# Linear attention and an expert layer on one core: second half of kv ahead of the denominators in batch 0, more idle products, and weight sums five tiles earlier

## The chip, the cores and the metric

The kernel runs on one core of a Trainium2 chip. The core has five engines with queues of their own: TensorE (PE in the profile; its weight loads are PEld), VectorE (DVE), ScalarE (ACT), GpSimd (POOL) and SyncE (SP). They meet through semaphores. Operands lie in SBUF; PE writes its results into PSUM, which has eight banks. The metric is the device time of one execution in microseconds (us), and of several runs the median.

## What is computed

Linear attention on 8 batches of 8 heads, 576 tokens and 64 channels, and then a dense layer on the 4608 tokens of 512 channels, with 2048 hidden channels:

```
phi(x) = where(x > 0, x, exp(x) - 1) + 1
kv  = einsum('bhsd,bhse->bhde', phi(k), v)
z   = sum(phi(k), axis=2)
x   = einsum('bhsd,bhde->bhse', phi(q), kv) / (einsum('bhsd,bhd->bhs', phi(q), z) + 1e-6)
h   = x @ w_in
out = (h * sigmoid(beta * h)) @ w_out
```

Inputs and output are float32; the kernel multiplies in bfloat16.

## The kernel before

The order of all work is written out by hand: each engine runs its instructions in the order in which the source issues them, and the framework adds the semaphore waits that the data need. A tile pool with a tag hands out its buffers in turn; a new tile waits until the last readers of its buffer are through.

The work is a pipeline over batches. For each batch, attention gives x (in the code xs, a tile of 128 tokens at a time), x is transposed to xT, an H phase makes 16 f tiles of h (128 hidden channels each, on 512 tokens) with the activation on ACT into g, and a Y phase multiplies g with w_out. While H and Y of block b run on PE, DVE, ACT and POOL prepare the attention of batches b + 1 and b + 2. The main loop hangs these pieces into the phases through two tables, `sh` for H and `sy` for Y: `at(sh, 9, f)` runs f after the f tile with number 9. Blocks 3 and up use a fast scheme in H (`h_fast`) that needs sums of parts of w_in; these are made once, by `h_w_sums(0)` in block 2: four DVE additions (lines 783 to 786). In blocks 1 and 2 the H phase is the plain one (`h_phase`). There, beside it, DVE also takes `kv_both` (line 231 copies kv out of PSUM), `numer_all` (lines 346 to 348, scaling of numerators of the next batch) and `g_parts` (lines 725 to 731, sums of g for the Y phase, each as soon as the last f tile of its four is there).

Batch 0 has no earlier work to hide behind, so it has an order of its own:

- SP loads q and k of batch 0 in halves of four heads; POOL loads v in two halves, after a small copy (`gate`) that waits for the first half of q, and then all weights in a row.
- `idle(n)` issues n products of a constant tile with itself into a bank that nobody reads. They compute nothing that is used. They stand at the start and wherever PE waits.
- phi of q, half by half (`phi_part`: exp on ACT, lines 169 and 175 on DVE), then its transposes on PE (`q_half`, `q_last`), which are copied to qT. bps is beta, transposed on PE.
- phi of k, half by half, `z_sums` (line 516) and `kv_first` (line 527), both on PE; `kv_mask` (line 536, two DVE instructions for each half) keeps the blocks of kv that belong to one head.
- zbd (line 554, two DVE instructions) is z in the same block form. The denominators are 20 small products of qT with zbd (line 564, tile dps), and `denom` (lines 571 and 572, an addition and a reciprocal on DVE) inverts them: once for the tiles 0 to 3 together, once for the last tile of 64 tokens.
- `numer_first(t)` makes the numerators of tile t on PE (line 583) and scales them on DVE (line 587). `x_first(t)` transposes the result on PE (line 382), and ACT copies it to xT (line 239). `h_first(t)` makes the part of the first four f tiles that belongs to tile t (line 402).

Two PSUM pools of four banks are in use during that: `hps` (`bank`) and `fps` (`bank1`). In the order of the source, the second half of kv comes after all denominators:

```
kv_first(0); z_sums(1); idle(1)
kv_mask(0); zbd
20 denominators; kv_first(1)
denom(tiles 0-3); kv_mask(1)
numer_first(0..2); denom(tile 4); x_first(0); numer_first(3); x_first(1); h_first(0); ...
```

Later lines that the text names: line 410 is the activation that writes g, line 162 the exp of later batches, line 986 the products of the Y phase, lines 1009 and 1010 DVE's sums u of them, line 1047 the gate copy that stands before the loads of later batches.

Of the kernel before, what the change touches and what calls it, by code (L numbers as in the profile page):

```python
# [8 lines left out]
F32 = mybir.dt.float32  # L9
BF16 = mybir.dt.bfloat16  # L10
ALU = mybir.AluOpType
# [5 lines left out]
def kernel(  # L17
# [10 lines left out]
    nc = tc.nc  # L28
# [4 lines left out]
    P = 128  # L33
    KC = DM // P
    FC = DFF // P
    G = 64
    J = S // G
    NT = 5
# [6 lines left out]
    consts = ctx.enter_context(tc.tile_pool(name="consts", bufs=1))  # L45
# [5 lines left out]
    def bank(name, shape=None, dt=F32):  # L51
        return hps.tile(shape or [P, 512], dt, tag="h", name=name)

    def bank1(name, shape=None, dt=F32):
        return fps.tile(shape or [P, 512], dt, tag="f", name=name)
# [17 lines left out]
    warm = consts.tile([P, 512], BF16, name="warm")  # L73
# [73 lines left out]

    warm_ps = bank("warm_ps")

    def idle(n):  # L150
        for _ in range(n):
            nc.tensor.matmul(warm_ps, warm[:, 0:P], warm, start=True, stop=True)

    def table(func):
        nc.scalar.activation(act0, warm[:, 0:1], func)  # L155
# [2 lines left out]
    st = {}  # L158
# [23 lines left out]
    def xin(b, a, pr):  # L182
        if b == 0:
            return x0f[pr if a == "q" else 2 + pr]
        return (xk if a == "k" else xq)[b % 2][:, 2 * pr : 2 * pr + 2]

    def phi_part(b, a, pr):
        x = xin(b, a, pr)
        phi_exp(b, a, pr, x)
        phi_relu(b, a, pr, x)  # L190
        phi_min(b, a, pr)
# [17 lines left out]
    def half(hh):  # L209
        return slice(hh * G, (hh + 1) * G)  # L210
# [32 lines left out]
    def q_half(b, pr, tp):  # L243
        for j in range(8):
            nc.tensor.matmul(
                tp.rearrange("p (t h i g) -> p t h i g", t=4, h=2, i=2)[:, j // 2, :, j % 2, :],
                st[b, "q"][:, pr, j, :], identity,
                is_transpose=True, start=True, stop=True, skip_group_check=True,
            )
# [35 lines left out]
    def rows_of(t):  # L285
        return P if t < NT - 1 else G

    def xs_tile(b, t):
        st[b, "xs", t] = xs_sb.rearrange("p i n -> p (i n)")[:, t * DM : (t + 1) * DM]
        n = rows_of(t)  # L290
        return st[b, "xs", t][:n].rearrange("p (i a d) -> p a i d", a=2, d=D)
# [188 lines left out]
            nc.vector.tensor_sub(ws[k][:, r], a, b)  # L480


    idle(11)
    beta_c = consts.tile([P, FC], F32)
    beta_m = consts.tile([P, FC], F32)
    rbeta = consts.tile([P, FC], F32)
# [5 lines left out]
    qtp = [bank1("qtp", [P, 1024], BF16) for _ in range(2)]  # L492
    phi_part(0, "q", 0)
    q_half(0, 0, qtp[0])
    idle(3)
    phi_part(0, "q", 1)
    q_half(0, 1, qtp[1])
    t8 = bank1("qtp8", [P, 2 * P], BF16)
    q_last(0, t8)
    bps = bank("bps", [P, FC])  # L500
    nc.tensor.matmul(bps, beta_row, ident16, is_transpose=True, start=True, stop=True)
    idle(4)
    x = xin(0, "k", 0)
    phi_exp(0, "k", 0, x)
    phi_relu(0, "k", 0, x)
# [5 lines left out]
    zbd = consts.tile([P, 2, 2, 2], BF16)  # L511

    def z_sums(pr):
        for j in range(J):
            for hh in range(2):
                nc.tensor.matmul(
                    zps[hh][:, pr : pr + 1], st[0, "k"][half(hh), pr, j, :], ones[half(hh)],
                    start=(j == 0), stop=(j == J - 1), skip_group_check=True,
                )
# [4 lines left out]
    def kv_first(pr):  # L524
        for j in range(J):
            for hh in range(2):
                nc.tensor.matmul(
                    kvp0[hh][:, pr * P : (pr + 1) * P],
                    st[0, "k"][half(hh), pr, j, :],
                    v0b[half(hh), 2 * pr : 2 * pr + 2, j, :],  # L530
                    start=(j == 0), stop=(j == J - 1), skip_group_check=True,
                )

    def kv_mask(pr):
        for hh in range(2):
            nc.vector.tensor_mul(
                kv0[:, hh, pr].rearrange("p (h d) -> p h d", h=2),
                kvp0[hh][:, pr * P : (pr + 1) * P].rearrange("p (h d) -> p h d", h=2),
                kvmask[:, hh, :, 0:D],
            )  # L540

    z_sums(0)
    idle(1)
    phi_part(0, "k", 1)
    q_copy(nc.scalar, 0, 1, qtp[1])
    q_copy_last(nc.scalar, 0, t8)
# [2 lines left out]
    kv_first(0)  # L549
    z_sums(1)  # L550
    idle(1)
    kv_mask(0)
    for hh in range(2):
        nc.vector.tensor_mul(
            zbd[:, hh], zps[hh][:, 0:2, None].to_broadcast([P, 2, 2]), kvmask[:, :, :, 0]
        )
    dps = bank("dps", [P, NT, 2, 2, 2])
    den0 = consts.tile([P, NT, 8], F32)
    rden0 = consts.tile([P, NT, 8], F32)
    for t in range(NT):  # L560
        n = rows_of(t)
        for hh in range(2):
            for pr in range(2):
                nc.tensor.matmul(
                    dps[:n, t, hh, pr], st[0, "qT"][:, pr, t, hh, 0:n], zbd[:, hh, pr, :],
                    start=True, stop=True, skip_group_check=True,
                )
    dv = dps.rearrange("p t a b c -> p t (a b c)")

    def denom(r, ts):  # L570
        nc.vector.tensor_scalar(den0[:r, ts], dv[:r, ts], 1e-6, None, ALU.add)
        nc.vector.reciprocal(rden0[:r, ts], den0[:r, ts])

    kv_first(1)
    denom(P, slice(0, NT - 1))
    kv_mask(1)

    def numer_first(t):
        n = rows_of(t)
        nps = bank1("nps0", [P, 2, 2, P])  # L580
        for hh in range(2):
            for pr in range(2):
                nc.tensor.matmul(
                    nps[:n, hh, pr], st[0, "qT"][:, pr, t, hh, 0:n], kv0[:, hh, pr, :],
                    start=True, stop=True, skip_group_check=True,
                )
        nc.vector.tensor_mul(
            xs_tile(0, t),
            nps[:n].rearrange("p a b (c d) -> p a (b c) d", d=D),
            rden0[:n, t].rearrange("p (a i) -> p a i", a=2)[:, :, :, None].to_broadcast(  # L590
                [n, 2, 4, D]
            ),
        )
# [5 lines left out]
    hp0 = []  # L599

    def h_first(t):
        if not hp0:
            hp0.extend(bank("h_ps") for _ in range(4))
        for ff in range(4):
            h_mm(xT[0], ff, hp0[ff], t * P, (t + 1) * P)

    for t in range(3):
        numer_first(t)
    denom(G, slice(NT - 1, NT))
    x_first(0, nc.scalar)  # L610
    numer_first(3)
    x_first(1, nc.scalar)
# [107 lines left out]
    def at(side, n, *fs):  # L720
        side.setdefault(n, []).extend(fs)
# [58 lines left out]
    def h_w_sums(fq):  # L780

        s, a = h_w[fq], lambda f, r: h_w_plain(fq, f, r)
        nc.vector.tensor_add(s[:, 0], a(1, 0), a(1, 1))
        nc.vector.tensor_sub(s[:, 1], s[:, 0], a(0, 0))
        nc.vector.tensor_sub(s[:, 2], a(0, 0), a(1, 0))
        nc.vector.tensor_sub(s[:, 3], a(0, 1), s[:, 1])
# [267 lines left out]
    for b in range(1, B + 1):  # L1054
        n, m = b + 1, b + 2
        sh, sy = {}, {}
        if b == 2 or b == B - 1:
            at(sh, 0, lambda: tail_copy(b))
        if n < B:
            at(sh, 0, lambda: next_loads(n))  # L1060
            if b > 2:
                at(sh, 0, lambda: tail_copy(b))
            at(sh, {1: 9, 2: 3}.get(b, 0), lambda: kv_both(n))
            at(sh, {1: 11, 2: 6}.get(b, 10), lambda: numer_all(n))
        if b == 1:
            at(sh, 4, lambda: w_sum(2))
            at(sh, 9, lambda: w_sum(1))
            at(sy, 0, lambda: w_sum(3))
        if m < B:
            at(sy, 0, lambda: phi_tile(m, "q"), lambda: phi_tile(m, "k"))  # L1070
            if b == 1:

                for pr in range(2):
                    at(sy, 0, lambda pr=pr: v_copy(nc.scalar, m, pr))
                for pr in range(2):
                    at(sy, 0, lambda pr=pr: phi_exp(m, "q", pr, xin(m, "q", pr)))
                    at(sy, 3 + 2 * pr, lambda pr=pr: phi_relu(m, "q", pr, xin(m, "q", pr)))
                    at(sy, 4 + pr, lambda pr=pr: phi_min(m, "q", pr))
                at(sy, 5, lambda: q_trans_dma(m))
                for pr in range(2):  # L1080
                    at(sy, 5, lambda pr=pr: phi_exp(m, "k", pr, xin(m, "k", pr)))
                    at(sy, 5 + pr, lambda pr=pr: phi_relu(m, "k", pr, xin(m, "k", pr)))
                    at(sy, 6, lambda pr=pr: phi_min(m, "k", pr))
                at(sy, 6, lambda: table(ACTF.Silu))
            else:
                at(sy, 0, lambda: phi_part(m, "q", 0))
                at(sy, 1, lambda: phi_part(m, "q", 1))
                at(sy, 1, lambda: q_trans_dma(m))
                at(sy, 4, lambda: phi_part(m, "k", 0))
                at(sy, 4, lambda: phi_part(m, "k", 1), lambda: table(ACTF.Silu))  # L1090
        if b == 2:
            at(sh, 9, lambda: h_w_sums(0))
        if b == B - 2:
            at(sy, 4, lambda: h_w_sums(2))
        if 2 <= b < B:
            at(sy, 6 if b < B - 2 else 0, lambda: h_x_sums(n))
        (h_phase if b < 3 else h_fast)(b, xT[b % 2] if b < B else xT_tail, sh)
        y_fast(b, sy)
# [30 lines left out]
```

## Time and profile before

| | |
|---|---|
| median of 3 runs | 273.99 us (273.18 to 275.07) |
| the profiled execution | 272.94 us, of which the span is 271.2 us |
| PE | 262.3 us busy, 97% of the span |
| DVE | 207.7 us, 77% |
| ACT | 168.6 us, 62% |
| POOL | 43.9 us, 16% |
| moved by DMA | 42.78 MB, 158 GB/s on average |

Times in the views are microseconds from the start of the span. A line of the timeline has the start, the time taken, the engine, the line of the source, the operation, what it writes and reads, the shape, and how many instructions are taken together; in brackets stands the idle time of the engine before it and what ended that. A q behind an engine's name is its instruction queue, which issues DMAs. A line of the view of waits has the waiting instruction, what it waited for, the sum, the number of times, and the longest.

Matmuls are pipelined. A row's duration runs to the modelled end of the last one, so of n matmuls each costs less than the row's time over n, and the distance from start to start is the price.

### The profile page before, as it was taken

The numbers are of one execution on the slowest core, as the hardware profiler recorded it, in microseconds if no ns is written. First come the engines' busy times: TensorE is split into PE (matmuls) and PEld (weight loads), VectorE is DVE, ScalarE is ACT, GpSimd is POOL, SyncE is SP. The second block draws the span as 40 slices with busy tenths as digits, with TensorE's granted clock in tenths as the row PEclk, the third lists the DMA queues.
The fourth block names the chain that finished last, engine by engine and source line by source line (L and its number), as shares of the span: only waits on it lengthen the run. The fifth ranks groups of instructions, "written<-read, shape, count | busy, mean of one in ns | idle before, by whom it ended". The sixth has DMA issues, their size and how long they took to land.

```text
span 271.2 us, 6775 instructions
## 1 busy us (share of the span) xinstructions
PE 262.3 (97%) x2852; PEld 180.9 (67%) x2857; DVE 207.7 (77%) x402; ACT 168.6 (62%) x237; POOL 43.9 (16%) x64
## 2 busy tenths in 40 slices
PE   7799999999999999999999999999999999999994
PEld 2475455445875487648865886588658866886793
DVE  4771785999895989689868986898778867856862
ACT  5738887976965776489448944885483038405810
POOL 5922004031003030330033003301000000000000
PEclk9999999999999999999999999999999999999999
DMA  7999999996718999999589668965504050023013
GB/s 250 234 206 348 242 396 239 287 212 214 136 19 177 272 178 126 265 233 99 87 219 264 112 93 229 248 117 86 158 2 89 0 155 4 0 55 102 0 41 116
DMA packets 48958, 42.78 MB, mean 158 GB/s; under 512 B 30352, under 2 KB 40736, under 8 KB 48928
## 3 DMA queue, kind: packets, MB, share of 16 engines
q0 software_dynamic: 13040, 23.40, 37.0%
q1 hardware_dynamic: 35568, 18.75, 32.8%
q8 instruction: 22, 0.36, 0.5%
q10 hardware_dynamic: 320, 0.20, 0.2%
q14 instruction: 8, 0.07, 0.1%
HBM read 36.71 MB, written 9.44 MB: 170 GB/s over the span
## 4 chain that ended last, share of the span: by engine, by line
PE 82%; DMA 10%; DVE 4%; issue 1%; ACT 1%; SPq 0%; POOL 0%; DVEq 0%; POOLq 0%; ACTq 0%
PE h_ps L402 31%; PE yd L986 10%; PE ya L986 9%; PE yb L986 8%; PE hc L820 5%; PE yc L986 5%; DMA xq<-in_q_dram 4%; PE y_ps L417 4%; PE hz L820 4%; DMA vf<-in_v_dram 2%; DMA qTd<-phi_q 2%; PE kvp L223 2%; PE nps L333 1%; DMA stage<-in_q_dram 1%; PE yb L958 1%; DVE phi_q L175 1%
## 5 line engine op out<-in xcount | busy, mean ns | idle before, releaser
L410 ACT ACTIVATE g<-h_ps,beta_c 128x512 bf16<-128x512 f32 x112 | 74.6, 689 | 60.6 <-PE h_ps L402 60.3
L402 PE MATMUL h_ps<-xT,w_in 128*128 128x512 bf16 (+1 forms) x464 | 97.6, 357 | 0.1
L402 PEld LDWEIGHTS <-w_in 128*128 128x128 bf16 x496 | 44.8, 98 | 40.7 <-issue 0.2
L986 PEld LDWEIGHTS <-stage 128*128 128x128 bf16 x480 | 47.0, 98 | 5.4
L986 PEld LDWEIGHTS <-g 128*128 128x128 bf16 x384 | 37.5, 98 | 6.4 <-issue 0.3
L986 PE MATMUL ya<-w_out,g 128*128 128x256 bf16 x256 | 30.6, 273 | 0.0
L241 POOL CAST vaug<-vf 128x1152 bf16<-128x1152 f32 x11 | 13.1, 1219 | 40.2 <-DMA vf<-in_v_dram 33.4
L348 DVE TENSOR_TENSOR xs_sb<-nps,rden 128x448 bf16<-128x448 f32 (+2 forms) x24 | 18.2, 758 | 0.8
L162 ACT ACTIVATE e<-xk 128x1152 bf16<-128x1152 bf16 (+1 forms) x15 | 16.7, 1161 | 1.2 <-DMA xk<-in_k_dram 1.2
L162 ACT ACTIVATE e<-xq 128x1152 bf16<-128x1152 bf16 x14 | 15.6, 1159 | 1.6 <-DMA xq<-in_q_dram 1.6
L155 ACT ACT_TABLE_LOAD x12 | 15.4, 1283 | 0.2
L986 PE MATMUL yd<-ws,g 128*128 128x256 bf16 x128 | 15.3, 272 | 0.2 <-DVE u L1010 0.2
L986 PE MATMUL yc<-ws,stage 128*128 128x256 bf16 x128 | 15.3, 273 | 0.0
L986 PE MATMUL yd<-ws,stage 128*128 128x256 bf16 x128 | 15.3, 273 | 0.0
L417 PE MATMUL y_ps<-w_out,g 128*128 128x512 bf16 x60 | 14.6, 379 | 0.3 <-issue 0.2
L175 DVE TENSOR_TENSOR phi_q<-e,r 128x1152 bf16<-128x1152 bf16 x16 | 12.1, 758 | 2.6 <-ACT e L162 1.5
L870 ACT ACTIVATE g<-hc,beta_c 128x512 bf16<-128x512 f32 x16 | 10.1, 682 | 6.4 <-DVE hc L856 6.4
L175 DVE TENSOR_TENSOR phi_k<-e,r 128x1152 bf16<-128x1152 bf16 x16 | 12.8, 803 | 1.2
L986 PE MATMUL yb<-ws,stage 128*128 128x256 bf16 x112 | 13.4, 273 | 0.0
L986 PE MATMUL yb<-w_out,stage 128*128 128x256 bf16 x112 | 13.4, 273 | 0.0
L820 PEld LDWEIGHTS <-w_in 128*128 128x128 bf16 x96 | 9.4, 98 | 4.5
L730 DVE TENSOR_TENSOR stage<-stage,g 128x1024 bf16<-128x1024 bf16 x16 | 11.9, 743 | 0.6
(135 smaller groups left out, 356.6 us busy)
## 6 DMA issues: line engine op xcount, KB each, us to landing
vf<-in_v_dram POOLq DMA_DIRECT2D x7, 1152.0 KB, 9.0
out_dram<-y SPq DMA_DIRECT2D x29, 256.0 KB, 3.9
xq<-in_q_dram POOLq DMA_DIRECT2D x7, 576.0 KB, 11.7
xk<-in_k_dram POOLq DMA_DIRECT2D x7, 576.0 KB, 14.9
w_in<-in_moe_w_in_dram POOLq DMA_DIRECT2D x4, 512.0 KB, 11.9
g<-in_moe_w_out_dram POOLq DMA_DIRECT2D x2, 1024.0 KB, 17.1
stage<-in_moe_w_out_dram POOLq DMA_DIRECT2D x2, 1024.0 KB, 21.1
stage<-in_q_dram SPq DMA_DIRECT2D x2, 576.0 KB, 4.2
```

The source lines that it names most:

```text
L155: nc.scalar.activation(act0, warm[:, 0:1], func)
L162: nc.scalar.activation(e, x, ACTF.Exp)
L175: nc.vector.tensor_tensor(st[b, a][:, pr].rearrange("p j (h d) -> p j h d", h=2), st[b, a, pr, "e"].rearrange("p h j d -> p j h d"), st[b, ...
L241: eng.tensor_copy(dst, src)
L348: nc.vector.tensor_mul(xs_sb[:, ils, v0 * D : v1 * D].rearrange("p i (u d) -> p i u d", d=D), pv[:, :, :, 0:D], rden[:, :, :, None].to_bro ...
L402: nc.tensor.matmul(hp[:, c0:c1].rearrange("p (t n) -> p t n", n=n), w_in_sb[ff // 4][:, kc, (ff % 4) * P : (ff % 4 + 1) * P], xm, start=(k ...
L410: nc.scalar.activation(g_sb[b % 2][:, ff, :], hp, ACTF.Silu, scale=beta_c[:, ff : ff + 1])
L417: nc.tensor.matmul(yp[:, c0:c1], g_sb[b % 2][:, ff, t * P : (t + 1) * P], w_out_sb[i][:, c, c0:c1], start=(ff == 0), stop=(ff == FC - 1), ...
L730: nc.vector.tensor_sub(gs[1][:, c], gs[0][:, c], g[:, c, 0:HM])
L820: nc.tensor.matmul(o, lhs[:, i, a * P : (a + 1) * P], m, start=(first and a == 0 and i == 0), stop=True, skip_group_check=True,)
L870: nc.scalar.activation(g_sb[b % 2][:, ff].rearrange("p (t n) -> p t n", t=2), src, ACTF.Silu, scale=beta_c[:, ff : ff + 1],)
L986: nc.tensor.matmul(ps[:, p * HM : (p + 1) * HM], lhs(c, p), rhs(c), start=(first and p == 0 and c == 0), stop=True, skip_group_check=True,)
```

## The change

There are three edits.

First, more idle products: 14 for 11 at the start, 5 for 3 after the first transposes of q, 7 for 4 after bps, 2 for 1 after the first sums of z, and two new ones before the first transposes of x. These last go to the bank of the first h tile, for which `idle` gets an argument.

Second, the order of batch 0. On DVE, zbd comes before the first masks of kv. On PE, the second half of kv comes before the 20 denominators. These go to two banks instead of one, tile 0 to the first and the other tiles to the second, and are inverted in three steps instead of two: tile 0, tiles 1 to 3 (between the scalings of tiles 0 and 1), and tile 4. The first four h tiles take two banks early and two later, because of the second bank for denominators.

Third, in block 2 the sums of w_in are issued after f tile 4 instead of f tile 9.

```diff
-    idle(11)
+    idle(14)
...
-    idle(3)
+    idle(5)
...
-    idle(4)
+    idle(7)
...
     z_sums(0)
-    idle(1)
+    idle(2)
...
     z_sums(1)
     idle(1)
-    kv_mask(0)
     for hh in range(2):
         nc.vector.tensor_mul(
             zbd[:, hh], zps[hh][:, 0:2, None].to_broadcast([P, 2, 2]), kvmask[:, :, :, 0]
         )
-    dps = bank("dps", [P, NT, 2, 2, 2])
...
+    kv_mask(0)
+    kv_first(1)
+
+    dps = [bank("dps", [P, NT, 8]) for _ in range(2)]
...
-    kv_first(1)
-    denom(P, slice(0, NT - 1))
+    for t in range(NT):
+        denom_mm(t)
     kv_mask(1)
+    denom(P, 0, 1)
...
+    hp0.extend(bank("h_ps") for _ in range(2))
     for t in range(3):
         numer_first(t)
-    denom(G, slice(NT - 1, NT))
+        if t == 0:
+            denom(P, 1, NT - 1)
+    idle(2, hp0[0])
+    denom(G, NT - 1, NT)
...
         if b == 2:
-            at(sh, 9, lambda: h_w_sums(0))
+            at(sh, 4, lambda: h_w_sums(0))
```

## The prediction

> **What bounds the kernel now.** I read three views in this order: the busy shares, what TensorE (PE) waits for, and the timeline of the two places that the change touches.
>
> The first lines of the page:
>
> ```profile
> PE 262.3 (97%) x2852; PEld 180.9 (67%) x2857; DVE 207.7 (77%) x402; ACT 168.6 (62%) x237; POOL 43.9 (16%) x64
> PEclk9999999999999999999999999999999999999999
> ```
>
> PE is busy 97% of 271.2 us, at full clock in every slice. So only PE's idle stretches can be shortened, or made longer. The view of PE's waits lists them:
>
> ```profile
> PE warm_ps L152 <- DVE warm L111: 1.5, 1, 1.5
> PE qtp L245 <- DVE phi_q L175: 0.9, 2, 0.5
> PE kvp L527 <- DMA vf<-in_v_dram: 0.9, 1, 0.9
> PE xtp L382 <- DVE xs_sb L587: 0.3, 1, 0.3
> PE zps L516 <- DVE phi_k L175: 0.3, 1, 0.3
> PE nps L583 <- DVE kv L536: 0.2, 1, 0.2
> PE yd L986 <- DVE u L1010: 0.2, 1, 0.2
> ```
>
> All but the last lie ahead of 17 us, where batch 0's attention is a chain. From the first h product at 16.93 on, PE has work nearly without a break. So the front edit is worth what it does to that 16.93, and the sums' edit at most the 0.2 us (0.17 in the timeline) of the last line.
>
> The front, from the timeline:
>
> ```profile
> 11.59 0.68 PE L527 MATMUL kvp<-vf,phi_k 64*128 64x128 bf16 x18 [0.91 <-DMA vf<-in_v_dram]
> 12.29 0.49 DVE L536 TENSOR_TENSOR kv<-kvp,kvmask 128x128 bf16<-128x128 f32 x2 [0.51 <-PE kvp L527]
> 12.70 0.22 DVE L554 TENSOR_TENSOR zbd<-zps,kvmask 128x4 bf16<-128x4 f32 x2
> 13.61 0.68 PE L527 MATMUL kvp<-vf,phi_k 64*128 64x128 bf16 x18
> 13.94 0.35 DVE L572 RECIPROCAL rden<-den 128x32 f32<-128x32 f32 x1
> 14.32 0.49 DVE L536 TENSOR_TENSOR kv<-kvp,kvmask 128x128 bf16<-128x128 f32 x2
> 15.11 1.89 DVE L587 TENSOR_TENSOR xs_sb<-nps,rden 128x512 bf16<-128x512 f32 x3 [0.31 <-PE nps L583]
> 16.93 1.05 PE L402 MATMUL h_ps<-xT,w_in 128*128 128x128 bf16 x16
> ```
>
> The chain to read: v's first half lands (11.55), kv, masks, second kv at 13.61, its masks, the first numerator, then three scalings (x3) back to back, 0.61 apart. The first h group needs two things: its xT copied by ACT (16.30 to 16.88), and PE past the second transposes (16.46 to 16.69), which need the second scaling. The copy is last, by 0.2 us.
>
> **Part 1, idle products.** Their price: 27 y products of the same form take 6.21, so (6.21 - 0.38) / 27 = 0.216 at full clock. Three more at the start: the eleventh begins at 5.61, so the transposes of q may begin at 5.61 + 4 x 0.216 = 6.48 instead of 6.39. These end 0.08 late; their reader, the copy of qtp on DVE, runs at 8.90. Five for three: 6.93 + 5 x 0.216 = 8.01, and PE waits for phi_q until 8.19. Seven for four: 9.02 + 7 x 0.216 = 10.53, so the sums of z start 0.22 late and end by 10.9. Two for one: to 11.2, and v lands at 11.55. All are hidden, the last by 0.39 us of the wait for v. Cost 0; uncovered, 11 products x 0.216 = 2.4.
>
> **Part 2, the order of the front.** Now DVE makes zbd first, then the masks of the first half, and PE runs the second kv before the denominators.
>
> - Second kv. It waits for v's second half and, bank by bank, for the masks. Behind it in PE's queue stand the 20 denominators, which before ran ahead of it. The half's DMA is the second of two issues (5.13 + 1.55 - 0.72 = 5.96), 7.0 us to landing: 13.0. GpSimd's wait for the same landing lets xk go at 13.29, an upper end. z's sums end at 12.48, so zbd starts at 12.50 (0.07 apart), masks at 12.64 and 12.85 (0.21 apart, 0.28 long), done at 13.13, released at 13.18 (PE follows a mask by 0.05 in this trace). Start 13.05, the second bank 13.18, last end 13.85 against 14.28: 0.43 gained.
> - Second masks: 13.88 to 14.37. PE meanwhile runs the 20 denominators (0.60) from 13.77 to 14.37 and turns to the numerators at 14.47 (0.10 to change, as at 13.61). So PE, not the masks, now sets the first numerator: done 14.85, and the first scaling starts at 14.89 instead of 15.11: 0.22 gained.
> - The split denominators. Tile 0's pair (sum and reciprocal, 0.15 + 0.20 by the 64x8 rows) runs 14.29 to 14.67, beside the numerators: hidden. But tiles 1 to 3 have a pair of their own behind the first scaling, and the second scaling waits for it. Before, one pair served four tiles at 13.71, where DVE was idle anyway. No row has 128x24. Between 64x8 (0.15, 0.20) and 128x32 (0.19, 0.35), by size: 0.18 + 0.30, and 0.03 of wait behind each. First scaling ends 15.58; pair 15.50 to 16.01; second scaling 16.05 to 16.73, against 15.72 to 16.40: 0.33 lost.
> - What is late next: the first transposes go at 15.64 (0.22 earlier; the two new idle products, 15.14 to 15.58, end before) and the first xT copy ends at 16.66. But the second transposes now start at 16.79, not 16.46, and the first h group behind them at 17.01. PE is last in place of ACT: 17.01 - 16.93 = **+0.08**.
> - Afterwards: third scaling ends 17.33, read at 18.3; the last pair frees the dps bank at 17.39, wanted by the fourth h tile at 17.68; the second xT copy ends at 17.80, wanted at 18.56. Nothing else is late.
>
> Ends: with the pair at 64x8 prices the h group starts at 16.81 (-0.12); at 128x32 prices 17.07, and with v at 13.29 17.17 (+0.24). I take the size-weighted +0.08.
>
> **Part 3, w_in's sums.** Four DVE additions, 91.30 to 92.76, go to the fifth f tile.
>
> ```profile
> 83.79 0.42 DVE L231 CAST kv_q<-kvp 128x260 bf16<-128x260 f32 x1
> 86.25 0.17 DVE L346 TENSOR_SCALAR den<-nps 128x7 f32<-128x7 f32 x1 [2.03 <-PE nps L333]
> 91.30 0.42 DVE L783 TENSOR_TENSOR h_w<-w_in 128x512 bf16<-128x512 bf16 x1
> 95.25 1.20 DVE L729 TENSOR_TENSOR stage<-g 128x1024 bf16<-128x1024 bf16 x1 [0.35 <-ACT g L410]
> 98.82 2.22 ACT L162 ACTIVATE e<-xq 128x1152 bf16<-128x1152 bf16 x2 [1.62 <-DMA xq<-in_q_dram]
> 103.39 0.81 PE L986 MATMUL yd<-ws,g 128*128 128x256 bf16 x6 [0.17 <-DVE u L1010]
> ```
>
> There DVE idles 2.03 us, from 84.21 to 86.25; the sums take 1.46 of it: hidden, 0.57 to spare. If that cover went, numerators of the next batch would be late by the excess, and their transposed x, issued from 89.81, is wanted at 107.0, in block 3's H. What is freed at 91.30 moves the first g sums about 1 us forward, but the second g sums wait for ACT's last g (95.22) as before, and the phi behind them waits for xq's landing (ACT's 1.62). So u, for which PE waits 0.17 at 103.39, stays where it is. Gain 0 of at most 0.17.
>
> One trace row speaks against the move: GpSimd's gate copy at 85.46, ahead of the loads of v, q and k, now falls beside the sums' last addition. At 61.22, beside DVE's L725 (to 61.53), it took 0.35 instead of 0.19. Yet from the gate's start to the load's issue it is 0.55 there and 0.54 at 85.46: the longer copy delayed nothing. The Trainium skill (SBUF — State Buffer, "Who interferes with whom") says that a DVE instruction with two SBUF inputs contends with a GpSimd instruction that reads SBUF, the second one blocking until the first is done. By that alone an estimate is up to 0.3 us more for the gate, with xq and PE's wait later by as much, and a sum of +0.4; the trace agrees on the longer copy, not on the later load. I take 0.
>
> **Sum.** 0 + 0.08 + 0 = +0.1 us. The profiled execution takes 272.94 us (271.2 of span, 1.7 around it), which gives 273.0; it is 1.05 below the median of the runs, 273.99, so I forecast the median at **274.1**. A measurement of this kernel can tell about 1% (2.7 us) from no change; the runs before lie 1.9 us apart.
>
> **The rivals.**
>
> 1. Slower: the idle products run cold and hold up the front. The trace has the step: products 0.43 apart until 5.52, then 0.22, 4.06 us after the first at 1.46. If the clock is granted later, fourteen at 0.43 end at 1.46 + 5.97 = 7.43 instead of 6.48. A microsecond of cold products costs half of one; the spare behind them (0.18 + 0.39) is used up when the grant comes 2 x 0.57 = 1.1 us later, after about 6.7. With a grant after twice the 4.06 us, at 9.58, the transposes end at 8.28, five products at 10.0, the second transposes and bps at 10.7, seven products at 12.2, z's sums and two products at 12.9: kv starts 1.3 after v, all of it on the path: 275.4. Eleven products would end at 6.15 and wait for phi_q as now. Against it: the one profile has the grant at 5.52. Chance 0.08. The Trainium skill (TensorE: Matmul & The Clock Gate, "Part 1") has the window behind the grant free-running and about 3.4 us long, so that its phase differs between executions; by that alone an estimate of the latest grant is 8.9, and of the cost 1.0. No run here shows a second phase.
> 2. Slower: v's second half lands late. Second kv had 0.56 us to spare (13.05 to 13.61); now denominators and all else queue behind it, and each microsecond after 13.14 counts. v's halves landed 1.5 apart; half a microsecond later makes +0.45: 274.4. Chance 0.12.
> 3. Faster: in other executions PE's waits ahead of 12 us (0.53, 0.26, 0.91) cost clock that this profile does not show, and the idle products save it. The most is the distance from the median to the lowest run: -0.8, 273.2. Against it: granted clock 1.00 throughout here. Chance 0.08.
> 4. Faster: the 0.22 of the first scaling survives, because the middle pair costs less than I take. Even at no cost at all, the second scaling comes at 15.50 and h at 16.71: -0.2, 273.8. Chance 0.12.
>
> The forecast itself, within 0.3 of 274.1: 0.6.
>
> **Range and chances.** The cases span 273.2 to 275.4. Three runs that lie 1.9 apart leave a median uncertain by some 0.5 on either side: 272.7 to 275.5. No case reaches 1%: same 0.95, slower 0.03 (rival 1 with rival 2 and more), faster 0.02.
>
> **What would show it.** Front: second kv at about 13.1, a first scaling at 14.9, DVE's 128x24 pair between the first and second scaling, and the first h group at 17.0. Idle products: the wait for v shrunk from 0.91 to about 0.4, kv still at 11.6. Sums: L783's additions at 84.3 under an otherwise unchanged 103.4. Wrong if the first h group starts outside 16.8 to 17.2, or if xq's landing in block 2 moves by more than 0.3.

## The result, and the profile after

The changed kernel takes 275.6 us (median of 11 runs, 274.23 to 276.21); the kernel before, run beside it, 274.05 (11 runs, 273.18 to 275.07). The ratio is 1.0057 (95% interval 1.0035 to 1.0078): slower by some 1.5 us. The forecast was 274.1. The profiled execution took 276.21 us with a span of 274.4, 3.2 us longer than the span before. That pair shows more than the medians do: 276.21 is the longest of the 11 runs, and the profile before, with 272.94, is shorter than any of the 11 beside it.

The page of the changed kernel, first line and the line of instruction transfers in its part 3:

```profile
PE 265.5 (97%) x2868; PEld 182.1 (66%) x2868; DVE 208.3 (76%) x404; ACT 168.6 (61%) x237; POOL 43.4 (16%) x64
...
q8 instruction: 22, 0.36, 0.5%
```

PE is busy 97% as before, and by 3.2 us more: the idle products are counted as work. So the share says nothing here, and the view by stretches is needed. For the kernel before (columns: stretch, its length, then busy time and instructions of PE, PEld, DVE, ACT, POOL, PE's clock, DMA share, GB/s):

```profile
0.00:17.00 17.00, 12.71 (x156) 7.20 (x158) 11.52 (x28) 9.57 (x13) 11.22 (x21) 1.00 0.99 235
83.00:90.00 7.00, 7.00 (x116) 3.42 (x105) 4.55 (x13) 4.24 (x7) 2.46 (x4) 1.00 0.94 200
205.00:220.00 15.00, 15.00 (x132) 12.68 (x131) 12.19 (x22) 2.28 (x5) 0.69 (x1) 1.00 0.34 78
```

The same stretches of the changed kernel:

```profile
0.00:17.00 17.00, 15.14 (x162) 8.18 (x162) 10.81 (x28) 9.28 (x12) 11.03 (x21) 1.00 1.00 240
83.00:90.00 7.00, 5.73 (x164) 3.20 (x164) 4.04 (x12) 3.09 (x5) 1.75 (x4) 1.00 0.85 192
205.00:220.00 15.00, 13.72 (x120) 11.55 (x119) 11.34 (x23) 3.03 (x5) 0.69 (x1) 1.00 0.20 40
```

Two new holes of 1.3 us stand where the kernel before had none, around 87 and around 215 us, far from the front. The view of PE's waits of the changed kernel names them:

```profile
PE warm_ps L152 <- DVE warm L111: 1.5, 1, 1.5
PE yd L998 <- DVE u L1022: 1.3, 1, 1.3
PE nps L335 <- DMA qTd<-phi_q: 1.3, 1, 1.3
PE xtp L384 <- DVE xs_sb L594: 0.6, 1, 0.6
PE kvp L529 <- DVE kv L538: 0.2, 1, 0.2
```

The waits for phi_q and v that were to hide the idle products are gone. The front, from the timeline of the changed kernel:

```profile
1.46 6.00 PE L152 MATMUL warm_ps<-warm 128*128 128x512 bf16 x14 [1.46 <-DVE warm L111]
7.29 0.61 PE L247 MATMUL qtp<-identity,phi_q 128*128 128x128 bf16 x8
9.63 1.68 PE L152 MATMUL warm_ps<-warm 128*128 128x512 bf16 x7
11.25 0.38 PE L518 MATMUL zps<-ones,phi_k 64*128 64x1 bf16 x18
12.10 0.68 PE L529 MATMUL kvp<-vf,phi_k 64*128 64x128 bf16 x18
13.49 0.86 PE L529 MATMUL kvp<-vf,phi_k 64*128 64x128 bf16 x18 [0.19 <-DVE kv L538]
14.95 0.20 DVE L578 RECIPROCAL rden<-den 128x8 f32<-128x8 f32 x1
15.42 0.69 DVE L594 TENSOR_TENSOR xs_sb<-nps,rden 128x512 bf16<-128x512 f32 x1 [0.27 <-PE nps L590]
16.23 0.30 DVE L578 RECIPROCAL rden<-den 128x24 f32<-128x24 f32 x1
16.64 1.29 DVE L594 TENSOR_TENSOR xs_sb<-nps,rden 128x512 bf16<-128x512 f32 x2
17.62 1.06 PE L404 MATMUL h_ps<-xT,w_in 128*128 128x128 bf16 x16
```

The first h group starts at 17.62 instead of 16.93: 0.69 lost. Of that, the first kv products start 0.51 later (12.10 against 11.59); from there to h it takes 5.52 instead of 5.34.

The Y phase of block 6, in which block 7's x is transposed and summed (called block 7 in what follows), the kernel before:

```profile
203.42 5.15 SPq L355 DMA_TRANSPOSE xT<-xs_sb  x4
210.06 0.43 DVE L805 TENSOR_TENSOR xs_sb<-xT 128x512 bf16<-128x512 bf16 x1 [0.96 <-DMA xT<-xs_sb]
...
212.47 0.69 DVE L1010 TENSOR_TENSOR u<-yd,u 128x512 f32<-128x512 f32 x1
213.22 1.91 PE L986 MATMUL yd<-ws,g 128*128 128x256 bf16 x16
```

and in the changed kernel:

```profile
205.26 5.16 SPq L357 DMA_TRANSPOSE xT<-xs_sb  x4
213.49 0.43 DVE L817 TENSOR_TENSOR xs_sb<-xT 128x512 bf16<-128x512 bf16 x1 [2.55 <-DMA xT<-xs_sb]
...
215.75 0.69 DVE L1022 TENSOR_TENSOR u<-yd,u 128x512 f32<-128x512 f32 x1
216.50 1.69 PE L998 MATMUL yd<-ws,g 128*128 128x256 bf16 x14 [1.28 <-DVE u L1022]
```

DVE waits 2.55 us for a transpose of x instead of 0.96; its sums u stand behind the sums of x that need it, and PE waits for u. The last of the four transposes was issued at 209.15 and landed at 213.37, 4.22 us later; in the kernel before it was issued at 207.31 and landed at 209.94, 2.63 later.

Block 2, the changed kernel:

```profile
84.83 0.42 DVE L795 TENSOR_TENSOR h_w<-w_in 128x512 bf16<-128x512 bf16 x1
87.82 0.83 PE L335 MATMUL nps<-kv_q,qTd 64*64 64x65 bf16 x72 [1.27 <-DMA qTd<-phi_q]
88.28 0.17 DVE L348 TENSOR_SCALAR den<-nps 128x7 f32<-128x7 f32 x1 [1.91 <-PE nps L335]
```

The moved sums of w_in stand where they were expected, with DVE idle behind them. PE waits for the second transpose of q: 15 of its 16 landings came by 86.18, the last at 87.78.

For these two profiles the account closes: 0.69 + 1.27 + 1.28 = 3.24 of 3.2 us.

### The profile page after: what moved, and what is told of

It is laid out like the page before. It is cut to its first block, busy times and chain, and to the rows that moved or that the text cites. A ratio compares the mean times of both kernels' runs of the same rounds, so it can differ in the third digit from the quotient of the medians.

```text
span 274.4 us, 6806 instructions
## 1 busy us (share of the span) xinstructions
PE 265.5 (97%) x2868; PEld 182.1 (66%) x2868; DVE 208.3 (76%) x404; ACT 168.6 (61%) x237; POOL 43.4 (16%) x64
## 4 chain that ended last, share of the span: by engine, by line
PE 88%; DVE 4%; DMA 4%; SPq 2%; issue 1%; DVEq 0%
PE h_ps L404 33%; PE yd L998 10%; PE ya L998 9%; PE yb L998 8%; PE hc L832 5%; PE yc L998 4%; PE y_ps L419 4%; PE hz L832 4%; PE warm_ps L152 3%; DMA qTd<-phi_q 2%; PE nps L335 2%; PE kvp L225 2%; DMA xT<-xs_sb 2%; PE yb L970 1%; SPq L357 1%; PE xtp L384 1%
## 5 line engine op out<-in xcount | busy, mean ns | idle before, releaser
L741 DVE TENSOR_TENSOR stage<-g 128x1024 bf16<-128x1024 bf16 x16 | 11.9, 743 | 2.3 <-ACT g L412 2.3
```

The costliest lines, as they stand in the source:

```text
L741: nc.vector.tensor_add(gs[0][:, c], g[:, c, HM:512], g[:, c2, HM:512])
```

## The experiments

Which of the three edits makes these two landings late? Nothing in the change touches the transposes. The theory that was left standing, C in the texts on record: PE's program is itself read by DMA. The 22 packets of q8 are 16 KB each, and the page counts 2857 weight loads before and 2868 after, each with a product (five of the products before left no record), so the program has some 5714 instructions before and 5736 after, about 260 to a packet (each of the 11 idle products is a weight load and a matmul). An insertion moves all later fetches against the work, and, so the theory, a fetch that starts too soon behind the issue of a transpose makes its landing late. The Trainium skill (Runtime: NRT & Kernel Launch, "Terms") has the instruction memory of each engine refilled in blocks of 16 KiB; the trace agrees with 0.36 MB in 22 packets. The rivals: the order of the front, the sums, the clock, or the mere time that the products take.

The kernel before, run beside each, is given with its own median, since it differs from chip to chip by some tenths.

### One part of the change at a time

The idle products alone (9 of the 11; the two before the first transposes of x belong to the new order), the order with its split denominators alone, the sums alone, each in the kernel before. The diffs are those of the change; the first one:

```diff
-    idle(11)
+    idle(14)
...
-    idle(3)
+    idle(5)
...
-    idle(4)
+    idle(7)
...
     z_sums(0)
-    idle(1)
+    idle(2)
```

> The kernel before with nine of the eleven new idle products (14, 5, 7 and 2) and nothing else; the two in the first h bank are left out. Theory A (cold products): the front alone is lengthened, by 0 if the clock is granted before about 6.7 us and by some 0.5 us if it is granted near 7.2; the first h group then starts at 16.9 to 17.5, and the median is 0 to 0.6 us above the kernel before. Theory C (instruction fetch): PE's program is 18 instructions longer ahead of everything, so the pieces in which it is read move against the transposing DMAs; stalls of about 1.3 us on a transpose appear in block 2 or block 7, and the median rises by 0.8 to 2 us. Theory B (the sums of w_in collide with transposes): nothing beyond A.

> The new order of batch 0 alone: zbd first, second kv ahead of the denominators, denominators in two banks and three steps; idle products and sums as before. Theory A: the first h group starts 0.1 to 0.2 us later than the 16.93 of before (0.18 by the distance from the first kv product to the first h product, 5.52 in the changed kernel against 5.34), and the median moves by 0.1 to 0.2 us. Theories B and C: the same, since PE has two instructions fewer or more at most and the sums stay at f tile 9; no stall of 1 us in block 2.

> The kernel before with the sums of w_in after f tile 4 and nothing else. Theory B: the sums, which now run beside the transposes of q in flight, make these land late; PE waits some 1.3 us for qTd in block 2, and the median rises by about 0.8 us or more. Theories A and C: no such wait, the last of the 16 landings of that transpose comes with the others, and the median stays within 0.3 us.

Measured: idle products 275.48 against 273.71, ratio 1.0077 (1.005 to 1.0103); order 273.63, 1.0006 (0.9982 to 1.003); sums 273.45, 0.9997 (0.9969 to 1.0025). PE's waits with the idle products alone:

```profile
PE yd L986 <- DVE u L1010: 1.3, 1, 1.3
PE nps L333 <- DMA qTd<-phi_q: 1.2, 1, 1.2
```

Both holes are back, while the first h group starts at 16.92, where it was before: the longer idle stretches cost the two late landings, although the front of this profile is no longer. The order alone and the sums alone have neither hole. The front with the order alone:

```profile
14.34 0.20 DVE L578 RECIPROCAL rden<-den 128x8 f32<-128x8 f32 x1
14.81 0.69 DVE L594 TENSOR_TENSOR xs_sb<-nps,rden 128x512 bf16<-128x512 f32 x1 [0.27 <-PE nps L590]
15.63 0.30 DVE L578 RECIPROCAL rden<-den 128x24 f32<-128x24 f32 x1
16.03 1.29 DVE L594 TENSOR_TENSOR xs_sb<-nps,rden 128x512 bf16<-128x512 f32 x2
17.02 1.06 PE L404 MATMUL h_ps<-xT,w_in 128*128 128x128 bf16 x16
```

The forecast had 14.89, the pair to 16.01, 16.05 and 17.01. The sums of w_in, alone, ran at 84.12 to 85.67, and u's reader on PE started at 103.33 (103.39 before): nothing gained, nothing lost.

### Instructions without time

Eleven products of one column, 22 PE instructions that take 0.3 us together, behind z's first sums in the kernel before; and the same eleven in the Y phase of the last block, where every fetch that matters has happened. The early ones:

```diff
     z_sums(0)
     idle(1)
+    for _ in range(11):
+        nc.tensor.matmul(warm_ps[:, 0:1], warm[:, 0:P], warm[:, 0:1], start=True, stop=True)
```

> The kernel before with eleven products of a single column, 22 PE instructions, where PE waits for v anyway: as many instructions more as in the changed kernel, but no time of PE. Theory C: fetch pieces move as in the changed kernel; stalls of about 1.3 us on transposing DMAs come in block 2, block 7 or both, and the median rises by 0.8 to 1.5 us with a front as before (first h group at 16.9). Theory A: no change, within 0.2 us. If stalls of that size come and go without any of the edits, they are chance (theory D), and each kernel's runs will spread as widely.

> The kernel before with the eleven products of one column ahead of the last Y phase instead of the front: as many PE instructions as in the changed kernel, but all fetches up to 240 us stay where they are. Theory C: no stall in block 2 or 7, median up by no more than 0.3 us (11 x 0.025). If more instructions cost time wherever they stand, or if the difference in e_shift was chance, the median rises by about 2 us as there.

Measured: early 275.8 against 273.71, ratio 1.0082 (1.0051 to 1.0112); late 273.8 against 273.9, 1.0011 (0.999 to 1.0032). The early ones did not lengthen the front (first h group at 16.59), but the time rose by 2.1 us, more than the expected 0.8 to 1.5. They made a hole in block 7, and none in block 2:

```profile
215.41 1.91 PE L988 MATMUL yd<-ws,g 128*128 128x256 bf16 x16 [1.56 <-DVE u L1012]
```

Another 0.74 us at 42.27 is a wait for ACT's copy of v, whose load landed later than in the kernel before; why, no run shows. So for block 7's hole neither the time of the products nor a later clock is needed (it came at 4.36 here), but their place ahead of the fetches is, and the order and the sums are out as its causes. In block 2 this profile has no hole, although the 22 instructions are there.

### Other numbers of instructions

Four kernels: the changed kernel again; the changed kernel with 17 of its idle products replaced by 134 of one column, so that the program is 256 instructions longer than before, about one 16 KB block (the trace has 23 packets in q8 instead of 22, so q8 does carry PE's program), and the fetches should be back in their place; 9 idle products fewer than before (18 instructions); and 5 products of one column (10 instructions) where the 11 had stood.

The edit of the second of these:

```diff
+    def narrow(n, ps=None):
+        ps = warm_ps if ps is None else ps
+        for _ in range(n):
+            nc.tensor.matmul(ps[:, 0:1], warm[:, 0:P], warm[:, 0:1], start=True, stop=True)
...
-    idle(5)
+    narrow(40)
...
-    idle(7)
+    narrow(55)
...
-    idle(2)
+    narrow(16)
...
-    idle(1)
+    narrow(8)
...
-    idle(2, hp0[0])
+    narrow(15, hp0[0])
```

> The changed kernel once more, for a second profile. Theory C: PE waits for qTd in block 2 or for u in block 7, or both, by over 1 us, as in the first profile; median 275.6 within 0.5. Front: the first h group at 17.0 if the clock is granted before about 6.7 us, up to 17.6 if later. Theory D (chance): neither stall, and other waits in their place.

> The changed kernel with 17 of its wide idle products (those of 5, 7, 2, 1 and 2) replaced by 134 products of one column, about as much time of PE (134 x 0.025 = 3.4 us for 17 x 0.22 = 3.7 us). PE's program is then 256 instructions, 16 KB, longer than the kernel before, one whole piece of the instruction queue, and the pieces are cut at the same work as in the kernel before. Theory C (place of the fetches): the stalls at about 87 and 215 us are gone, the median is within 0.7 us of the kernel before (the front's own part), and below the changed kernel by over 1 us. If the number of instructions matters otherwise (each costs time), it is slower than the changed kernel. If the edits themselves make the stalls (theories B and D), they stay, and the median stays at some 1.5 us above the kernel before.

> The kernel before without nine of its idle products (those of 3, 4, 1 and 1): 18 PE instructions fewer. Theory C: fetches come later against the work, by about 0.4 us (the changed kernels have them 0.5 us earlier for 18 to 22 instructions more); in block 7 the fetch falls behind the landing of xT, no stall of over 1 us there and at block 2, median the same as before or up to 0.8 us below. If the idle products keep the clock (rival 3 of the prediction), the granted clock falls somewhere in the first 20 us, and the front is longer by 1 us or more.

> The kernel before with 5 products of one column (10 PE instructions, no more than 0.15 us of PE time) after the first idle product behind z's first sums: a smaller dose of the shift that 11 of them (22 instructions) gave. Theory C: the fetch in block 7 starts about 0.2 us earlier against the transpose's issue, 2.3 us behind it, which is the edge (2.46 and more was not delayed, 2.13 and less was): the wait for u in block 7 in some of its executions or none, median between 273.8 and 275.6. Rival (each added instruction costs the same): 273.8 + 10/22 x 2.0 = 274.7. The trace decides rather than the median: with the fetch at 2.46 or later no wait, at 2.13 or earlier a wait of 1.3.

Measured: the changed kernel again 275.47 against 273.9, ratio 1.0073 (1.0041 to 1.0105), with the hole in block 7 (1.5) and none in block 2. 9 fewer: 274.27, 1.0028 (1.0004 to 1.0051), neither hole, but the clock at half from 10.82 to 17.64 us and a first h group 0.85 later. 5 narrow products: 273.73 against 273.32, 1.0018 (1.0001 to 1.0035), no hole in its profile, one of its 12 runs at 275.2. 256 more: 276.47, 1.0114 (1.0077 to 1.0151), a miss by time (within 0.7 of the kernel before was expected): the narrow products did not keep PE's clock. The clock in 40 slices, with 256 more instructions:

```profile
PEclk9959999999999999999999999999999999999999
```

It was at half from 13.52 to 20.35 us, and the first h group started 3.0 us later (19.90); in that time PE also stood 1.34 us, up to 15.52, for nothing that the profile shows. But PE waits in neither of the two places there, although its program holds more added instructions than any other: for block 7, the number does not matter, where the blocks fall does.

The trace has the start of each DMA packet, so of each fetch too. For the last transpose of x in block 7, in every profile, sorted by the time from its issue to the start of the fetch (us; the last packet is the transpose's own):

| kernel | PE instructions more | fetch after issue | last packet after issue | landing after issue |
|---|---|---|---|---|
| 9 idle products fewer | -18 | 3.61 | 2.17 | 2.63 |
| sums alone | 0 | 3.00 | 2.17 | 2.63 |
| 11 narrow, late | 22 behind it | 2.70 | 2.17 | 2.63 |
| zbd first (below) | 0 | 2.65 | 2.17 | 2.63 |
| order alone | 0 | 2.57 | 2.17 | 2.63 |
| before | 0 | 2.53 | 2.17 | 2.63 |
| 256 more | 256 | 2.45 | 2.17 | 2.62 |
| 5 narrow | 10 | 2.42 | 2.17 | 2.61 |
| three edits and both covers (below) | 18 | 2.22 | 3.09 | 15 of 16 by 2.71, one 4.28 |
| idle products alone | 18 | 2.13 | 3.17 | 4.24 |
| changed, both covered (below) | 22 | 2.12 | 3.46 | 4.34 |
| changed | 22 | 2.11 | 3.15 | 4.22 |
| three edits (below) | 18 | 2.10 | 3.14 | 4.21 |
| 11 narrow, early | 22 | 2.03 | 3.64 | 4.49 |
| changed, again | 22 | 1.32 | 3.83 | 4.40 |
| changed, sums of x later (below) | 22 | 1.22 | 3.18 | 3.77 |

There is one edge, between 2.22 and 2.42, and no exception in 16 profiles. A landing takes 2.63 undisturbed; a fetch that starts 0.4 or more before that makes it 1.1 to 1.9 late.

The packets show how. From 1 us ahead of that issue to 5 us behind it, the trace of every profile holds nothing but the packets of the transposes (some 1590, of 4 or 256 bytes) and the one fetch of 16 KB, so no other transfer is in the way. Undisturbed, the last of them starts at 2.17. With a fetch at 2.03 to 2.13, five to twelve packets of 256 bytes and two of 4 start only when the fetch has ended (in the changed kernel 2.11 + 0.89 = 3.00, the first of them at 2.98), and all 16 landings are late. With a fetch at 2.22 only two packets of 4 bytes are left to wait, until 3.08, and one landing is late. At 2.42 none is left. With a fetch at 1.2 or 1.3, some twenty packets take 1.0 to 2.0 us each instead of less than 0.1, and some 135 of 256 bytes start only when the fetch has ended. So the edge is the end of the transpose's own packets.

### Taking PE's wait away, and leaving the late landing

If the late landing is the cost, it must cost nothing where nobody waits for it. In the changed kernel, block 7's sums of x are issued behind DVE's sums u; PE's program stays the same, instruction for instruction:

```diff
-            at(sy, 6 if b < B - 2 else 0, lambda: h_x_sums(n))
+            at(sy, 6 if b < B - 2 else 3 if b < B - 1 else 0, lambda: h_x_sums(n))
```

> The changed kernel with one line moved: in block 6's Y phase the four sums of x for block 7 (DVE L817) are issued after DVE's two sums u (L1021, L1022) instead of ahead of them. PE's program is the same instruction for instruction, so the pieces of its program are fetched where they were. Theory C (a fetch falls between the issue and the landing of block 7's fourth transpose, the landing comes 1.6 us late, the sums of x on DVE wait for it, u waits behind them, PE waits for u): the landing stays late (4.2 to 4.5 us after its issue), but u no longer stands behind it, and PE's wait of 1.3 to 1.5 us at about 215 is gone: median 1.3 below the changed kernel's, 274.2 (273.9 to 274.6). Rival (the time is lost by a clock that comes later or by the longer front): nothing changes, 275.5.

Measured 274.77 against 273.32, ratio 1.0059 (1.0043 to 1.0075). The timeline:

```profile
213.48 0.69 DVE L1021 TENSOR_TENSOR u<-yc,r 128x512 f32<-128x512 f32 x1 [2.64 <-PE yc L998]
214.21 0.69 DVE L1022 TENSOR_TENSOR u<-yd,u 128x512 f32<-128x512 f32 x1
214.81 0.42 DVE L817 TENSOR_TENSOR xs_sb<-xT 128x512 bf16<-128x512 bf16 x1
214.95 1.91 PE L998 MATMUL yd<-ws,g 128*128 128x256 bf16 x16
```

The landing stays late (3.77 us) and PE's wait is gone, as expected. The time is above the expected 273.9 to 274.6, and the ratio is that of the changed kernel, which the rival expected. The profile has the other hole,

```profile
PE nps L335 <- DMA qTd<-phi_q: 1.1, 1, 1.1
```

and a front 0.88 longer than before (first h group at 17.81), which make up its whole 273.2 of span (271.2 + 1.1 + 0.9). So the profile speaks for the theory, while its time alone does not decide between the two.

So the second hole was covered too. The numerators that need block 2's transpose of q go two f tiles later:

```diff
-            at(sh, {1: 11, 2: 6}.get(b, 10), lambda: numer_all(n))
+            at(sh, {1: 11, 2: 8}.get(b, 10), lambda: numer_all(n))
```

> The changed kernel with both waits covered: block 7's sums of x behind DVE's u (as in the run with that one line moved), and in block 2 the numerators of the next batch after f tile 8 instead of 6, some 1.7 us later, so that a landing of the second transpose of q that comes 1.6 late is still there in time. PE's idle products and the whole front are those of the changed kernel. Theory C (the two late landings cost 1.3 each where PE meets them, the rest is the front): PE's waits at about 87 and 215 are both gone, in all runs, and what is left is the front's 0.4 to 0.9: median 0.5 to 0.9 above the kernel before, ratio 1.002 to 1.0035; the runs in one group instead of two. Rival (what is lost follows from the idle products in another way, for instance a clock or a front that the profiles don't show): ratio stays at 1.0057 or more.

Measured 273.97 against 273.54, ratio 1.0006 (0.9984 to 1.0028). Both landings were late in its profile (block 2 by 1.55 us, block 7 at 4.34 after its issue), and PE met neither:

```profile
88.25 0.83 PE L335 MATMUL nps<-kv_q,qTd 64*64 64x65 bf16 x72
...
104.40 1.91 PE L998 MATMUL yd<-ws,g 128*128 128x256 bf16 x16 [0.44 <-DVE u L1022]
...
214.15 1.91 PE L998 MATMUL yd<-ws,g 128*128 128x256 bf16 x16
```

With every edit of the change in place, its loss is gone but for 0.4 us, and the front alone is 0.6 longer in this profile (first h group at 17.54). The ratio is below the expected 1.002 to 1.0035, but its interval reaches into it; the kernel before loses some runs to the clock, which this one does not (below), and that may be why.

### Versions that might beat both

zbd ahead of the first masks in the kernel before, with one pair of denominators as before and no instruction more; then three edits: the same with the longer idle stretches and the sums of x behind u; then that with the later numerators and the early sums of w_in.

```diff
-    kv_mask(0)
     for hh in range(2):
         nc.vector.tensor_mul(
...
         )
+    kv_mask(0)
```

> The kernel before with one edit: zbd ahead of the first masks of kv on DVE; one pair of denominators for tiles 0 to 3 as before, the second half of kv behind the denominators as before, PE's number of instructions the same. By the durations of the trace: denominators at 12.70 instead of about 13.0, second kv at 13.40 instead of 13.61, first h group at about 16.73 (16.93 before). No wait for u in block 7. Median 0.2 below the kernel before, ratio 0.999 (0.997 to 1.001).

> The kernel before with three edits: zbd ahead of the first masks; the 18 PE instructions of the longer idle stretches (14, 5, 7, 2 for 11, 3, 4, 1); and block 7's sums of x behind u as in the run with that one line moved. Theory C: the transpose in block 7 lands late as in the run with idle products alone, but PE does not wait for it; the clock is kept (granted clock 0.997 or more in its runs, where the kernel before has 0.986 to 0.994 in a third of them), and the first h group comes 0.2 earlier: median 273.3, ratio 0.998 (0.995 to 1.000). If a landing of block 2's second transpose of q is late, as with the idle products alone, PE waits 1.2 there and the median is 274.5.

> The kernel before with zbd ahead of the first masks, the 18 PE instructions of the longer idle stretches, both waits covered as in the run beside this one, and w_in's sums after f tile 4 (they leave the stretch that the later numerators need). In the run without the last two edits five runs lay at 273.1 to 273.4 and six at 274.2 to 274.6. Theory C: the upper group was the late landing of block 2's second transpose of q, and it is gone: all runs in the lower group, median 273.1, ratio 0.998 (0.996 to 1.000). Rival (the two groups have another cause): two groups again, median 273.2 to 274.5.

Measured: zbd first 273.11 against 273.32, ratio 1.0002 (0.9985 to 1.0018), its first h group at 16.84 instead of the expected 16.73: z's sums ended when they had, and the denominators began 0.09 earlier, not 0.3. From the first kv product to the first h group it takes 5.55, against 5.34 before, so a median 0.2 lower, as expected, is no sign of a gain. With all three edits 274.21, 1.0023 (1.0007 to 1.004), not the expected 273.3: five runs at 273.1 to 273.4 and six at 274.2 to 274.6. The idle products alone had 1.0077, and zbd by itself gave nothing, so the difference speaks in time for block 7's wait. With the two further edits 274.04 against 273.54, 1.0005 (0.9981 to 1.0029), and the runs from 272.96 to 275.07: the upper ones, expected to go, are still there. Its profile, one of them, tells why:

```profile
87.20 0.19 POOL L1047 COPY gate<-qTd 128x1 bf16<-128x1 bf16 x1 [12.81 <-DMA qTd<-phi_q]
...
99.73 2.22 ACT L162 ACTIVATE e<-xq 128x1152 bf16<-128x1152 bf16 x2 [2.47 <-DMA xq<-in_q_dram]
...
104.30 1.91 PE L986 MATMUL yd<-ws,g 128*128 128x256 bf16 x16 [1.01 <-DVE u L1010]
```

The late transpose of q (1.6) also holds GpSimd's gate copy, 87.20 instead of 85.46, and with it the loads of the next batch: xq landed at 99.65 instead of 98.74, phi and then u came later, and PE waits 1.01 there instead of 0.17. The wait was moved, not removed. None of these versions is faster than the kernel before by what was measured.

## Why the prediction was wrong

**Part 1, the idle products at cost 0: wrong, and the step that failed.** The prediction counted their time against PE's waits. Two things were missing. First, they are also 22 instructions of PE's program, and that alone, with next to no time, costs a hole of 1.3 to 1.6 us in block 7: shown by the eleven narrow products early against the same ones late, and by the packets that wait for the fetch. Block 2's hole is tied to the longer idle stretches too, but its cause is open: of the seven profiles of kernels with the longer idle stretches three have the other hole, two more have the late landing with the wait covered, and two have neither; of the other nine none has it. Second, the term itself was too small. From the second transposes of q to kv it takes 3.29 us at full clock with the longer stretches (8.28 to 11.57 with the idle products alone); the prediction had 8.19 to 11.2, 3.0 (by its own prices the two products behind z's sums end at 11.3). So the cover of 0.39 behind the last idle products was 0.1, and it hangs on v: in the three edits, where v's first half landed at 10.52, kv starts at 11.90, and with zbd first, where it landed at 10.53, at 11.29.

**Rival 1, cold products: seen in the profile, and small.** The clock came at 7.17 instead of 5.52; fourteen products end at 7.29, the second transposes of q run at 8.82, and kv starts at 12.10 though v had landed at 11.62. Over the 16 profiles the clock came between 4.33 and 7.41. By the rival's own price (half of what the grant is past 6.7) that is 0.24; it was 0.48, as the cover was smaller. (By the same price a grant at 8.9, the latest that the prediction takes there, would cost 1.1, not 1.0.) It is no explanation of the rest: with the grant at 4.82 the idle products alone cost the same.

**Part 2, the order: right in mechanism, the size a little off.** +0.08 was forecast. The order alone has its first h group at 17.02, 0.09 later than before, but that is luck: v's first half landed 0.09 earlier there. From the first kv to the first h it takes 5.52, as in the changed kernel, against 5.34: +0.18. The split denominators do what was said: the first scaling is earlier, and the second waits for the pair of tiles 1 to 3 (in the changed kernel it starts at 16.64 behind a reciprocal that ends at 16.53, a wait of 0.11 where 0.03 was taken). v's second half (rival 2) held PE for 0.23 in the order alone, and its weight loads for 0.24 in the changed kernel. **Rival 4** did not come.

**Part 3, the sums: right.** Hidden, no gain: 0.9997. With the sums alone, the gate copy beside them took 0.21 and xq landed at 98.68 (98.74 before), so the estimate from the rule on the shared port (+0.4) is not borne out.

**Rival 3, the idle products keep the clock: its mechanism is real, and hidden under the loss.** Beside the experiments, 25 of 101 runs of the kernel before had a mean granted clock below 0.995, and of the 65 runs of kernels with the longer idle stretches (the changed one among them) none was below 0.997. In the kernel before such runs are longer, by 0.3 to 1.7 us by the medians of the four groups of runs (in one 274.4 against 273.3), which raises the mean over all runs by some 0.3. With 9 idle products fewer every one of 12 runs had 0.988 or less. So the idle products do keep the clock, and they lose more by the late landings that came with them.

**The range** ended at 275.5, because no case had a cost outside the front and the two edited places. Both signs of being wrong that the prediction named appeared: the first h group at 17.62, outside 16.8 to 17.2, and xq's landing in block 2 at 100.62 instead of 98.74, since the gate copy ahead of its load waits for the late transpose of q (87.89 instead of 85.46). That it came out the same within 1%, as forecast with 0.95, is no credit to the sum: the loss is clear of no change.

## What to carry to other kernels

A filler instruction is not free just because its engine was idle: it shifts everything in the program behind it, and where instruction blocks are fetched is part of the schedule. When a profile shows a loss far from the edit, compare issue and landing of the DMAs there, and then the starts of the instruction fetches in both traces; a dozen instructions without work, early and late, tell such a shift from the cost of the work itself within two runs. A cure that holds wherever the fetch falls is slack behind the landing: one line that took DVE's u out from behind a landing removed a wait that the change had only exposed.

## What the hardware showed

A fetch of 16 KB of PE's program takes 0.9 to 2.4 us in the traces. If it starts between 1.2 and 2.13 us after the issue of a DMA transpose that lands 2.63 after its issue when undisturbed, all 16 landings come 1.1 to 1.9 us late; at 2.22, one of 16 came 1.6 late; from 2.42 on, none. In block 2, where 15 landings came 0.26 to 0.52 behind the start of the fetch, one of 16 came 1.6 late in five of seven profiles with the longer idle stretches, and on time in the other two, and in the nine of the other kernels, several at the same distance (the kernel before 0.27 to 0.45). So the place of the fetch alone does not separate them there. The Trainium skill (DMA: Bandwidth & Descriptors, "Queues, rings and completion order") has each DMA engine take turns between its queues, a packet at a time; the packets in block 7 that start only when the fetch has ended fit that, though the trace does not name the DMA engine of a packet. But 1.6 us is more than the 0.9 that this fetch itself takes: the last landing comes 0.46 after the last packet starts when undisturbed, and 0.6 to 1.2 after it when late. Why, and why all 16 are late when data packets of some wait, stays open, as does why block 2's landing differs between executions.

Products of one column do not keep PE's clock: 134 of them in the place of 17 full ones, and it fell to half for 7 us.
